# Threshold attention and SwiGLU on one core: the first batch's planned order, its spread, and the opening scores

## The chip, the cores and the metric

The kernel runs on one core of a Trainium2 chip. The metric is the device time of one execution in microseconds (us). The kernel before took 1339.34 us (median of 3 runs, 1338.71 to 1340.52). The core's engines each work through an instruction queue of their own: TensorE (PE in the profile, its weight loads PEld), VectorE (DVE), ScalarE (ACT) and GpSimd (POOL); SyncE (SP) issues most of the DMAs. They meet only at semaphores.

## What is computed

Eight batches of eight heads, 576 tokens, head dimension 64. Per head, scores below the row's maximum less tau are masked out; then softmax and the product with v. The 4608 x 512 result goes through a SwiGLU block with d_ff = 1536. Cut from the reference:

```python
scores = scale * np.matmul(q, k.transpose(0, 1, 3, 2))
thresh = np.max(scores, axis=-1, keepdims=True) - tau
scores = np.where(scores >= thresh, scores, -1000000000.0)
scores = scores - np.max(scores, axis=-1, keepdims=True)
attn = np.exp(scores)
attn = attn / (np.sum(attn, axis=-1, keepdims=True) + 1e-09)
x = np.matmul(attn, v)          # then heads side by side: (4608, 512)
g = x @ w_gate
out = (g * (1.0 / (1.0 + np.exp(-g))) * (x @ w_val)) @ w_out
```

All of it is float32.

## The kernel before, in words

The work has three stages.

**The first batch, order written out by hand (0 to about 130 us).** Heads go in four pairs. For each pair the queries are cut in tiles of 128 rows: first two early tiles of each pair, then the rest (two of 128 rows and a last one of 64). The loop at L801 runs over pairs and tiles. `scores` (L489) is a generator: it issues the score products of both heads of a tile (`sc`, L498; keys of all 576 tokens, two PSUM banks for a head), takes each row's maximum on VectorE (L515, `nm`), yields, has ScalarE form threshold and exponential (L518, L519), yields, has VectorE mask and sum (L522), add up (L524) and invert (L525, `ri`), and scales. `flip_steps` (L549) then turns the tile on TensorE (`tp`, `end`, L568 and L572), ScalarE copies it out (L575, L582), and `attend_tile` (L586) multiplies by v (`xa`). The pool `ps_s` has room for the scores of one tile (two buffers of two banks); the other four banks are the pool `ps_f`, handed out in turn by `bank` (L292). `run_idle` (L301) issues products whose result nobody reads, before the first scores and again while the first tile is on the other engines.

Ahead of that loop, L749 to L754 set up the inputs: tau's DMA is issued on ScalarE's queue, then `fetch_qk(0)` issues four loads of k and four of q, five on SP and three on ScalarE's queue; a load takes one of eight semaphores in turn, and one whose semaphore is in use waits for the load that holds it. `prepare` (L717) transposes k, scales the first queries by a factor formed from tau, and transposes them.

Between the tiles, pieces of the weights are loaded and turned into a two-part form (`split_weights`, `shift_weights`, `join_weights`; L361, L362 on ScalarE; L381, L388 on VectorE; L398 on GpSimd).

**Batches two to eight, order set by a planner (from about 127 us).** `Plan` (L28) keeps an assumed time for TensorE (`plan.t`) and for every other engine (`plan.free`). Each piece of work on VectorE, ScalarE, GpSimd or SP is a job with an engine, an assumed duration, jobs that it waits for, a rank, and possibly a lag (time after its end until others can go on). The planner issues jobs in the order in which they could start by these times; so the assumed times set only the order of the instructions in each queue. TensorE's own order is written out. `take` (L919) picks the bank that comes free first by the plan. `shares` (set at L2423, for the tail alone) makes the planner stretch jobs of VectorE and GpSimd that run side by side, by the factors `SLOWED` (L34).

Attention here goes in slots: each pair has three, so a batch has 12 (slots s = 0 to 11 are batch two, 12 to 23 batch three). `slot_scores` issues 64 small products in one block (L2088; about 1.65 us, both buffers of `ps_s`), and `slot_rest` makes the jobs behind them: maxima (L2109, L2111), exchange between row groups on ScalarE (L2123) or on VectorE (L2117) by a table, threshold (L2130), exponentials (L2134), masks (L2136), sums (L2145, L2151), inverse (L2152), scaling on ScalarE (L2164) or GpSimd (L2161), transposes (L2166). The next block of scores needs the banks that the last masks release. After three slots `attend` (L2188) multiplies by v. Between the blocks of scores TensorE works on the SwiGLU block of the batch before; for the first batch that is `plain_group` (L1400: `pg`, `pv`), which goes in steps of four 128x128x256 products. Tables say how many steps go into which slot and who does what: `PLAIN` and `CH0` for batch two, `GV_FIRST` for batch three, `FIRST_POOLED` (how many of a slot's scalings go to GpSimd) and `FIRST_MAX_BY_ACT` (whose exchange is done by ScalarE) for both. `rest_of_weights` (L960) makes jobs of the weight pieces that are not done by then (L982, L985 on ScalarE; L992, L994 on VectorE; L996 on GpSimd), with an assumed landing time `landed` for loads that are already on their way.

The hand-over is in the loop at L2369: at s = 0 the last tile of the first stage is finished by hand, and then the plan's clocks are set:

```python
plan.t += 2.4
plan.free.update(DVE=2.0, ACT=2.5)
```

**The tail (from about 1130 us).** The last gate and value products come from `Whole` (L2574: `pa`, `pb`, `pe`, `sc` by bank), in twelve groups, then the output products from `Deep` (L1797, L1806). A gate's seven partial products are copied by ScalarE or added by VectorE (`Seven.fill`, L1300 and L1302; L2646, L2656) and folded by four additions on GpSimd or VectorE (`Seven.fold`, L1304); then come Tanh on ScalarE (L2624), a multiply on VectorE (L2626), and the gate's multiply.

Of the kernel before, what the change touches and what calls it, by code (L numbers as in the profile page):

```python
# [10 lines left out]
F32 = mybir.dt.float32  # L11
# [3 lines left out]
ALU = mybir.AluOpType  # L15
# [12 lines left out]
class Plan:  # L28
# [2 lines left out]

    HOP, PIPE = 0.08, 0.22
    PATIENCE = 0.2
    SLOWED = {"DVE": 0.45, "POOL": 0.2}  # L34
    AGE = 12.0

    def __init__(self):
# [120 lines left out]
def kernel(  # L158
# [40 lines left out]
    qkp = ctx.enter_context(tc.tile_pool(name="qkp", bufs=2))  # L199
    stp = ctx.enter_context(tc.tile_pool(name="stp", bufs=4))  # L200
    ps_s = ctx.enter_context(tc.tile_pool(name="ps_s", bufs=2, space=bass.MemoryType.PSUM))
    ps_f = ctx.enter_context(tc.tile_pool(name="ps_f", bufs=1, space=bass.MemoryType.PSUM))
    hbm = ctx.enter_context(tc.tile_pool(name="hbm", bufs=1, space=bass.MemoryType.DRAM))
    ctx.enter_context(tc.manual_schedule())

# [92 lines left out]
    def give_back(ps):  # L298
        turns.append(taken.pop(id(ps))[0])

    def run_idle(n):  # L301
        ps = bank("idle")
        for _ in range(n):
            nc.tensor.matmul(ps[:, 0:TC], ones[:, 0:P], ones, start=True, stop=True)
        give_back(ps)

    FW = 384
    TW = 2 * FW
# [177 lines left out]
    def statistics(*names):  # L486
        return [stp.tile([P, 2 * NU3, 2] if x == "mx" else [P, 2 * NU3], F32, name=x) for x in names]

    def scores(seg, t):  # L489
        qT, kT = seg["qT"], seg["kT"]  # L490
        q0 = t * P - seg["q0"]
        if t < NT:
            pss = [ps_s.tile([P, 2, 512], F32, name="sc") for _ in range(2)]
            for h, hs in enumerate(heads):
                cut_ = D if turned(t) and h == 1 else 0
                for n, lo, to in [(0, 0, D), (0, D, SH), (1, 0, SH)] if cut_ else [(0, 0, SH), (1, 0, SH)]:
                    at_ = (n * SH + lo - cut_) % S
                    nc.tensor.matmul(pss[h][:, n, lo:to], qT[hs, q0:q0 + P], kT[hs, at_:at_ + to - lo],  # L498
                                     start=True, stop=True)
        else:  # L500
            pss = [ps_s.tile([P, 2, 512], F32, name="sc")]
            for n, h in ((0, 0), (1, 1), (1, 0), (0, 1)):
                hs = heads[h]
                nc.tensor.matmul(pss[0][hs, n, 0:SH], qT[hs, q0:q0 + D], kT[hs, n * SH:(n + 1) * SH],
                                 start=True, stop=True)
        nm, th, ri, tot = statistics("nm", "th", "ri", "tot")
        sm = sums[0]
        sums.rotate(1)
        m = len(pss)
        scs = [ps[:, :, 0:SH] for ps in pss]  # L510
        both = pbufs[0].rearrange("p h s -> p (h s)")[:, KM:KM + P]
        ps = [pbufs[0][:, x, :].rearrange("p (n s) -> p n s", n=2) for x in range(m)]
        pbufs.rotate(1)
        for x in range(m):
            nc.vector.tensor_reduce(out=nm[:, x:x + 1], in_=scs[x], axis=AX.XY, op=ALU.max, negate=True)  # L515
        yield
        for x in range(m):
            nc.scalar.activation(th[:, x:x + 1], nm[:, x:x + 1], AF.Identity, bias=cut, scale=-1.0)  # L518
            nc.scalar.activation(ps[x], scs[x], AF.Exp, bias=nm[:, x:x + 1])  # L519
        yield  # L520
        for x in range(m):
            nc.vector.scalar_tensor_tensor(out=ps[x], in0=scs[x], scalar=th[:, x:x + 1], in1=ps[x],  # L522
                                           op0=ALU.is_ge, op1=ALU.mult, accum_out=sm[:, x, 0:1])
        nc.vector.tensor_reduce(out=tot[:, 0:m], in_=sm[:, 0:m, 0:3:2], axis=AX.X, op=ALU.add)  # L524
        nc.vector.reciprocal(out=ri[:, 0:m], in_=tot[:, 0:m])  # L525
# [220 lines left out]
        ready.append(unit)  # L746
        left[0] += cost(unit)

    run_idle(6)  # L749
    nc.scalar.dma_start(out=tau_s, in_=tau.partition_broadcast(P))  # L750
    fetch_qk(0)
    prepare(segs[0])
    fetch_qk(1)
    nc.scalar.activation(junk, minus2, AF.Exp)  # L754
# [31 lines left out]
    def steps(n, x, point):  # L786
        for what in STEPS.get((n, x, point), ()):
# [9 lines left out]
            else:  # L797
                {"scale": scale_next, "turn": turn, "split": split_weights, "shift": shift_weights,
                 "join": join_weights}[what]()

    for n, seg in enumerate(segs[:2 * NP]):  # L801
        early_slots[0] = n < NP
        if n >= NP:
            seg["v"] = segs[seg["i"]]["v"]
        for x, t in enumerate(seg["tiles"]):
            assert n < NP or seg["i"] in turned_rests
            go = scores(seg, t)
            next(go)
            steps(n, x, "maxima")
            if n >= NP:  # L810
                join_weights(1)
            if not n and not x:
                run_idle(6)
            next(last, None)
            box = []
            if n < NP:
# [45 lines left out]
            gates()  # L862
            last = go
            steps(n, x, "end")
            if n >= NP and x == len(seg["tiles"]) - 2 and n + 1 < len(segs):
                prepare(segs[n + 1])

# [92 lines left out]
    def rest_of_weights():  # L960

        todo = [(dst, None, place, lo) for dst, place, lo in split] + [(dst, None, place, None) for dst, place in fetched]
        landed = 6.3
        todo += [(dst, srcs, place, None) for dst, srcs, place in wpieces]
        done, joins = {}, []
        for n, (dst, srcs, place, lo) in enumerate(todo):
# [323 lines left out]
    class Seven(Buf):  # L1290
# [13 lines left out]
        def fold(self, eng, rank, *deps):  # L1304

            y = self.place.rearrange("p (x q) -> p x q", q=P)
            tt, took, less = (dve_tt, 0.36, 0.23) if eng == "DVE" else (pool_tt, 0.73, 0.46) if tail[0] else (pool_tt, 0.75, 0.44)
            twice = lambda x: y[:, x:x + 1].broadcast_to((P, 2, P))
            j = job(eng, took, tt(y[:, 1:3], twice(0), y[:, 1:3], ALU.add), *deps, rank=rank)
            j = job(eng, took, tt(y[:, 0:7:6], twice(2), y[:, 5:7], ALU.add), j, rank=rank)  # L1310
            j = job(eng, less, tt(y[:, 2], y[:, 0], y[:, 3], ALU.add), j, rank=rank)
            return job(eng, took, tt(y[:, 4:6], twice(6), y[:, 4:6], ALU.add), j, rank=rank, lag=0.3 if tail[0] else 0.0)

    class Flat:

# [988 lines left out]
    LAST_GV, LAST_PLAIN, LATE_V = 9, 8, 10  # L2304
    HELD = 4
    GV = {1: 3, 2: 6, 3: 4, 4: 6, 5: 7, 6: 3, 7: 5, 8: 7, 9: 0}
    GV_FIRST = {1: 5, 2: 8, 3: 2, 4: 5, 5: 7, 6: 2, 7: 5, 8: 7, 9: 0}
    CH = {0: 2, 1: 3, 10: 4, 11: 4}
    POOLED = {NS: 2, 0: 3, 1: 1, 2: 1, 3: 3, 4: 3, 5: 2, 6: 1, 7: 2, 8: 1}
    MAX_BY_ACT = (0, 1, 3, 4, 5, 6, 8, 9)  # L2310
    FIRST_POOLED = {0: 2, 4: 1, 5: 1, 8: 1, 9: 1, 11: 2, 12: 2, 13: 3, 15: 3, 16: 3, 17: 2, 19: 2, 20: 2, 22: 3, 23: 3}
    FIRST_MAX_BY_ACT = (1, 3, 6, 9, 10, 11, 12, 13, 14, 18, 20, 21)
    CD = {0: 1, 1: 1, 9: 2, 10: 2, 11: 2}
    PLAIN = {0: 3, 1: 5, 2: 6, 3: 2, 4: 5, 5: 5, 6: 3, 7: 3}
    CH0 = {7: 1, 8: 3, 9: 2, 10: 3, 11: 3, 12: 2}

    def begin_outputs(c):
# [51 lines left out]
    for s, (n, x) in enumerate((n, x) for n in range(len(halved)) for x in range(NU3)):  # L2369
# [6 lines left out]
        if s == 0:  # L2376
# [1 line left out]
            attend_tile()  # L2378
            next(last, None)
            flip()  # L2380
            plan.t += 2.4
            plan.free.update(DVE=2.0, ACT=2.5)
        elif s == 1:
            box = []
            m = pe(1.0, lambda: attend_tile(lambda *y: box.extend(y)))
# [358 lines left out]
```

## Time and profile before

| what | us |
|---|---|
| runs of the kernel before (3) | 1338.71, 1339.34, 1340.52 |
| the profiled execution's own time | 1340.89 |
| its span, first to last instruction | 1338.8 |
| TensorE with a running matmul | 1324.7 (99%) |
| VectorE, GpSimd, ScalarE busy | 1095.3, 940.2, 900.5 |
| from the first instruction to the first score products | 7.88 |
| first score products to the first block of slot scores | 7.88 to 126.77 |
| granted TensorE clock, mean | 0.999 |

The profile shows one execution. A row of the timeline tells when a group of equal instructions began (us from the span's start), how long it took in all, its engine, its line, what it writes and reads, how many they were, and in brackets how long the engine had been idle before and what ended that. A matmul of 128x256 in float32 runs as two passes, and each pass is a row of the trace: at full clock a pass of 256 columns starts every 0.216 us, and one of 128 columns every 0.112 us. The end of a matmul is modelled, so for a pause I look at the distance between starts. The view of stretches gives, for each stretch of time, what every engine was busy and the granted clock.

### The profile page before, as it was taken

How to read it: one execution, taken by the hardware profiler on the slowest of the kernel's cores; microseconds unless marked ns; L12 is line 12 of the kernel's file. 1: busy time of each engine (PE TensorE's matmuls, PEld its weight loads, DVE VectorE, ACT ScalarE, POOL GpSimd, SP SyncE). 2: the span in 40 equal slices, each digit the busy share in tenths (PEclk: the TensorE clock that was granted, in tenths of full speed). 3: DMA queues.
4: the chain of work that ended last, by engine and by line, in shares of the span. 5: the costliest groups of instructions: out<-in, count | busy, mean ns of one | idle time of the engine just before them, and what ended most of it. 6: DMA issues, size and time to landing. Idle time of an engine off the chain costs nothing. (4 is left out here: it accounts for less than half of the span.)

```text
span 1338.8 us, 41744 instructions
## 1 busy us (share of the span) xinstructions
PE 1324.7 (99%) x16298; PEld 1122.5 (84%) x16298; DVE 1095.3 (82%) x2904; ACT 900.5 (67%) x2345; POOL 940.2 (70%) x1124
## 2 busy tenths in 40 slices
PE   8999999999999999999999999999999999999998
PEld 6777777787887888888888888888888888999998
DVE  6889898888887788888888887888788888767886
ACT  6898776767755777787677777777777774444300
POOL 2588497565685969857895779677975798866720
PEclk9999999999999999999999999999999999999999
DMA  8753424356557653656365736655475627565341
GB/s 183 198 193 96 81 60 133 123 150 178 154 167 217 174 172 94 198 170 220 76 201 170 233 103 188 186 164 154 110 218 142 217 69 226 160 199 185 96 170 40
DMA packets 230884, 209.81 MB, mean 157 GB/s; under 512 B 167968, under 2 KB 185376, under 8 KB 223008
## 3 DMA queue, kind: packets, MB, share of 16 engines
q1 hardware_dynamic: 226768, 206.22, 52.2%
q8 instruction: 129, 2.11, 0.6%
q10 hardware_dynamic: 3920, 0.92, 0.3%
q14 instruction: 67, 0.55, 0.1%
HBM read 169.08 MB, written 38.01 MB: 155 GB/s over the span
## 5 line engine op out<-in xcount | busy, mean ns | idle before, releaser
L2136 DVE SCALAR_TENSOR_TENSOR pall<-sc,th,pall 128x288 f32<-128x288 f32 x504 | 244.1, 514 | 39.9 <-ACT pall L2134 20.8
L2134 ACT ACTIVATE pall<-sc,nm 128x288 f32<-128x288 f32 x504 | 232.6, 497 | 35.0 <-DVE pall L2136 34.8
L1167 PE MATMUL pb<-xall,big 128*128 128x256 f32 x864 | 205.9, 381 | 0.0
L2166 DVE STREAM_TRANSPOSE pall<-pall 128x576 f32<-128x576 f32 x252 | 188.0, 763 | 19.8 <-ACT pall L2164 9.8
L948 POOL TENSOR_TENSOR big<-big 128x128 f32<-128x128 f32 (+3 forms) x226 | 168.0, 752 | 50.9 <-ACT big L1302 22.1
L2164 ACT ACTIVATE pall<-pall,ri 128x288 f32<-128x288 f32 x386 | 178.3, 527 | 26.0 <-DVE ri L2152 25.0
L1167 PEld LDWEIGHTS pb<-xall,big 128*128 128x128 f32 x864 | 161.4, 190 | 23.6 <-issue 2.2
L948 POOL TENSOR_TENSOR hall<-hall,tmp 128x512 f32<-128x512 f32 x80 | 102.2, 1279 | 86.7 <-DVE hall L1226 66.9
L2109 DVE TENSOR_REDUCE mx<-sc 128x2 f32<-128x576 f32 x168 | 125.7, 748 | 41.9 <-PE sc L2088 41.6
L2088 PE MATMUL sc<-kT,qT 64*32 64x288 f32 (+1 forms) x5376 | 145.3, 345 | 1.1 <-DVE pall L2136 1.1
L1167 PE MATMUL pa<-xall,big 128*128 128x256 f32 x576 | 137.8, 382 | 0.0
L2088 PEld LDWEIGHTS sc<-kT,qT 64*32 64x32 f32 x5376 | 96.0, 106 | 49.4 <-issue 8.6
L2188 PE MATMUL xa<-pall,vall 64*32 64x288 f32 x4032 | 128.7, 404 | 0.0
L1167 PEld LDWEIGHTS pa<-xall,big 128*128 128x128 f32 x576 | 108.0, 190 | 17.2 <-issue 2.5
L2188 PEld LDWEIGHTS xa<-pall,vall 64*32 64x32 f32 x4032 | 74.0, 107 | 46.9 <-issue 4.3
L2161 POOL TENSOR_SCALAR pall<-pall,ri 128x288 f32<-128x288 f32 x118 | 59.4, 514 | 51.9 <-DVE ri L2152 51.6
L2145 ACT COPY sums<-sums 32x6 f32<-32x6 f32 x336 | 66.6, 198 | 29.2 <-DVE pall L2136 24.0
L1167 PE MATMUL pe<-xall,big 128*128 128x256 f32 x352 | 83.9, 381 | 0.0
L2111 DVE TENSOR_REDUCE mx<-sc 128x1 f32<-128x288 f32 x168 | 75.0, 447 | 0.0
L1167 PEld LDWEIGHTS pe<-xall,big 128*128 128x128 f32 x352 | 66.4, 190 | 10.2 <-ACT xlast L2200 0.7
L948 POOL TENSOR_TENSOR hall<-hall 128x384 f32<-128x384 f32 (+2 forms) x69 | 70.3, 1035 | 0.8
L948 POOL TENSOR_TENSOR big<-hall 128x384 f32<-128x384 f32 (+2 forms) x69 | 65.6, 974 | 4.3 <-PE pa L1167 4.2
(401 smaller groups left out, 3062.1 us busy)
## 6 DMA issues: line engine op xcount, KB each, us to landing
big<-sums_hbm SPq DMA_DIRECT2D x30, 1280.0 KB, 7.5
big<-sums_hbm SPq DMA_DIRECT2D x30, 1024.0 KB, 7.3
vall<-in_v_dram SPq DMA_DIRECT2D x112, 144.0 KB, 4.0
big<-sums_hbm SPq DMA_DIRECT2D x54, 256.0 KB, 3.4
sums_hbm<-big SPq DMA_DIRECT2D x36, 256.0 KB, 3.6
out_dram<-big SPq DMA_DIRECT2D x32, 256.0 KB, 3.0
qT<-in_q_dram SPq DMA_DIRECT2D x112, 72.0 KB, 4.2
kT<-in_k_dram SPq DMA_DIRECT2D x112, 72.0 KB, 3.0
```

The costliest lines, as they stand in the source:

```text
L948: nc.gpsimd.tensor_tensor(out=out, in0=a, in1=b, op=op)
L1167: nc.tensor.matmul(ps[:, i], w[:, k_, i * P:(i + 1) * P], x[:, k_, :], start=first and i == k_ == 0, stop=True, skip_group_check=True)
L2088: nc.tensor.matmul(pss[h][(slice(g * G, (g + 1) * G), *part)], qT[hs, col:col + G], kT[hs, c * SH + keys[0]:c * SH + keys[1]], start=True, ...
L2109: rs.append(job("DVE", 0.72, lambda n=n, tile_=tile_: nc.vector.tensor_reduce(out=mx[:, n:n + 2, 0], in_=tile_[:, :, 0:SH], axis=AX.X, op= ...
L2111: rs.append(job("DVE", 0.42, lambda n=n, tile_=tile_: nc.vector.tensor_reduce(out=mx[:, n + 2:n + 3, 0], in_=tile_[:, :, SH:SH + SQ], axis ...
L2134: ej = job("ACT", 0.42, lambda x=x, n=n: nc.scalar.activation(ps[x], scs[x], AF.Exp, bias=nm[:, n:n + 1]), ej, masks.get((h, u - 1)), rank=0)
L2136: masks[x] = job("DVE", 0.45, lambda x=x, n=n: nc.vector.scalar_tensor_tensor(out=ps[x], in0=scs[x], scalar=th[:, n:n + 1], in1=ps[x], op0 ...
L2145: nc.scalar.copy(sm[g * G:(g + 1) * G, 0:m, 1], sm[o * G:(o + 1) * G, 0:m, 0])
L2161: scaled.append(job("POOL", 0.48 if seg["i"] >= 3 * NP else 0.4, lambda x=x, n=n: nc.gpsimd.tensor_scalar(out=x, in0=x, scalar1=ri[:, n:n ...
L2164: scaled.append(job("ACT", 0.46, lambda x=x, n=n: nc.scalar.activation(x, x, AF.Copy, scale=ri[:, n:n + 1]), rj, rank=rank))
L2166: seg["turned"].append(job("DVE", 0.72, lambda both=both: nc.vector.transpose(out=both, in_=both), *scaled, rank=rank))
L2188: nc.tensor.matmul(holds[a].ap()[x * G:(x + 1) * G, 0:SH].rearrange("d (i q) -> d i q", q=G), vr[rs, h, j, ds], p[rs, h, :, j, :], start=( ...
```

## The change

Six edits.

1. **Opening.** The pool `ps_f` is opened only after the first tile. Until then its four banks hold the scores of the first tile (`first_pool`), so that the first two tiles have banks of their own. The scores of the second tile are issued right behind those of the first; its maxima are taken when its turn comes (`later`). The idle products write to a part of the first tile's bank that the scores leave free: 224 columns wide instead of 256, six and then four instead of six and six.
2. **Maxima.** In `scores`, a maximum is issued right behind its head's products instead of behind both heads'.
3. **Loads.** `fetch_qk(0)` comes ahead of tau's DMA.
4. **Hand-over.** The plan's clocks are set to other values, GpSimd's too, and the two banks that were given back last are marked as busy until ScalarE's assumed time. The loads on their way are assumed to land at 8.0 instead of 6.3.
5. **Spread.** The tables `PLAIN`, `GV_FIRST`, `FIRST_POOLED` and `FIRST_MAX_BY_ACT` get other entries.
6. **Tail.** The lag of a fold is 0.6 instead of 0.3, and the factor of GpSimd beside VectorE 0.3 instead of 0.2.

The diff, cut to its core:

```diff
-    SLOWED = {"DVE": 0.45, "POOL": 0.2}
+    SLOWED = {"DVE": 0.45, "POOL": 0.3}
...
-    ps_f = ctx.enter_context(tc.tile_pool(name="ps_f", bufs=1, space=bass.MemoryType.PSUM))
...
-    def run_idle(n):
-        ps = bank("idle")
+    def run_idle(n, ps):
         for _ in range(n):
-            nc.tensor.matmul(ps[:, 0:TC], ones[:, 0:P], ones, start=True, stop=True)
-        give_back(ps)
+            nc.tensor.matmul(ps[:, 1, SH:512], ones[:, 0:P], ones[:, 0:512 - SH], start=True, stop=True)
...
-    def scores(seg, t):
+    def scores(seg, t, pss=None, later=False):
...
+        def maximum(x):
+            nc.vector.tensor_reduce(out=nm[:, x:x + 1], in_=pss[x][:, :, 0:SH], axis=AX.XY, op=ALU.max, negate=True)
...
+                if not later:
+                    maximum(h)
...
+        yield
...
-        for x in range(m):
-            nc.vector.tensor_reduce(out=nm[:, x:x + 1], in_=scs[x], axis=AX.XY, op=ALU.max, negate=True)
+        if later or t >= NT:
+            for x in range(m):
+                maximum(x)
         yield
...
-    run_idle(6)
+    first_pool = tc.tile_pool(name="first", bufs=1, space=bass.MemoryType.PSUM)
+    in_first = first_pool.__enter__()
+    first_pss = [in_first.tile([P, 2, 512], F32, name=f"first{h}") for h in range(2)]
+    run_idle(6, first_pss[0])
+    fetch_qk(0)
     nc.scalar.dma_start(out=tau_s, in_=tau.partition_broadcast(P))
-    fetch_qk(0)
...
+    begun = deque([scores(segs[0], 0, first_pss)])
...
-            go = scores(seg, t)
+            go = begun.popleft() if begun else scores(seg, t)
+            if (n, x) != (0, 1):
+                next(go)
+            if (n, x) == (0, 0):
+                begun.append(scores(seg, seg["tiles"][1], later=True))
+                next(begun[0])
             next(go)
...
-                run_idle(6)
+                run_idle(4, first_pss[0])
...
+            if not n and not x:
+                first_pool.__exit__(None, None, None)
+                ps_f = ctx.enter_context(tc.tile_pool(name="ps_f", bufs=1, space=bass.MemoryType.PSUM))
...
-        landed = 6.3
+        landed = 8.0
...
-            return job(eng, took, tt(y[:, 4:6], twice(6), y[:, 4:6], ALU.add), j, rank=rank, lag=0.3 if tail[0] else 0.0)
+            return job(eng, took, tt(y[:, 4:6], twice(6), y[:, 4:6], ALU.add), j, rank=rank, lag=0.6 if tail[0] else 0.0)
...
-    GV_FIRST = {1: 5, 2: 8, 3: 2, 4: 5, 5: 7, 6: 2, 7: 5, 8: 7, 9: 0}
+    GV_FIRST = {1: 5, 2: 8, 3: 2, 4: 5, 5: 7, 6: 2, 7: 6, 8: 6, 9: 0}
...
-    FIRST_POOLED = {0: 2, 4: 1, 5: 1, 8: 1, 9: 1, 11: 2, 12: 2, 13: 3, 15: 3, 16: 3, 17: 2, 19: 2, 20: 2, 22: 3, 23: 3}
-    FIRST_MAX_BY_ACT = (1, 3, 6, 9, 10, 11, 12, 13, 14, 18, 20, 21)
+    FIRST_POOLED = {0: 2, 1: 2, 4: 1, 5: 1, 6: 2, 8: 1, 9: 2, 11: 3, 12: 3, 13: 3, 15: 3, 16: 3, 17: 2, 19: 2, 20: 2, 22: 3, 23: 2}
+    FIRST_MAX_BY_ACT = (1, 2, 3, 6, 9, 10, 11, 12, 14, 15, 17, 20, 21)
...
-    PLAIN = {0: 3, 1: 5, 2: 6, 3: 2, 4: 5, 5: 5, 6: 3, 7: 3}
+    PLAIN = {0: 4, 1: 4, 2: 6, 3: 3, 4: 4, 5: 5, 6: 3, 7: 3}
...
-            plan.t += 2.4
-            plan.free.update(DVE=2.0, ACT=2.5)
+            plan.t += 1.8
+            plan.free.update(DVE=2.7, ACT=4.4, POOL=5.7)
+            for n_ in list(turns)[-2:]:
+                j = Job("ACT", 0.0, None, 0, 0.0, 0.0)
+                j.end = plan.free["ACT"]
+                banks[n_].jobs.append(j)
```

More of the change, by code (lines that the diff above doesn't have):

```diff
@@ L487, in statistics @@
         return [stp.tile([P, 2 * NU3, 2] if x == "mx" else [P, 2 * NU3], F32, name=x) for x in names]
-    def scores(seg, t):
+    def scores(seg, t, pss=None, later=False):
         qT, kT = seg["qT"], seg["kT"]
         q0 = t * P - seg["q0"]
+        nm, th, ri, tot = statistics("nm", "th", "ri", "tot")
+        def maximum(x):
+            nc.vector.tensor_reduce(out=nm[:, x:x + 1], in_=pss[x][:, :, 0:SH], axis=AX.XY, op=ALU.max, negate=True)
         if t < NT:
-            pss = [ps_s.tile([P, 2, 512], F32, name="sc") for _ in range(2)]
+            pss = pss or [ps_s.tile([P, 2, 512], F32, name="sc") for _ in range(2)]
             for h, hs in enumerate(heads):
@@ L505, in scores @@
                                  start=True, stop=True)
-        nm, th, ri, tot = statistics("nm", "th", "ri", "tot")
+        yield
         sm = sums[0]
```

## The prediction

> **What bounds the kernel now.** I read the page first: is one engine full all the way, or does each stretch have its own limit?
>
> ```profile
> PE 1324.7 (99%) x16298; PEld 1122.5 (84%) x16298; DVE 1095.3 (82%) x2904; ACT 900.5 (67%) x2345; POOL 940.2 (70%) x1124
> ```
>
> TensorE is the bound: 14.1 us of the 1338.8 are without a running matmul. So a change is worth only the TensorE pauses that it closes (and the slow matmuls before the clock rises). Next I read TensorE's rows of the timeline for pauses of over 0.3 us, and the rows of the other engines around each. Three places are touched by the diff.
>
> *The start* (timeline, 0 to 40 us; columns: start, time, engine, line):
>
> ```profile
> 7.88 2.13 PE L498 MATMUL sc<-pall,qT 64*128 64x288 f32 x8 [2.05 <-DVE cap L734]
> ...
> 9.94 3.62 PE L304 MATMUL idle<-pall 128*128 128x256 f32 x12
> 10.02 1.42 DVE L515 TENSOR_REDUCE nm<-sc 128x1 f32<-128x576 f32 x2 [1.77 <-PE sc L498]
> ...
> 13.49 1.27 PE L498 MATMUL sc<-pall,qT 64*128 64x288 f32 x8
> 13.63 0.17 DVE L525 RECIPROCAL ri<-tot 128x2 f32<-128x2 f32 x1
> ...
> 14.76 1.42 DVE L515 TENSOR_REDUCE nm<-sc 128x1 f32<-128x576 f32 x2 [0.96 <-PE sc L498]
> ...
> 18.05 1.94 PE L498 MATMUL sc<-pall,qT 64*128 64x288 f32 x8 [0.94 <-DVE pall L522]
> ```
>
> TensorE fills 9.94 to 13.56 with idle products, because the second tile's scores need banks that the first tile's masks release only at 13.4. So VectorE, done with tile one at 13.80, waits 0.96 us for tile two, and the scores of tile three (18.05) wait on that chain.
>
> *The hand-over to the planner* (timeline, 123 to 144 us):
>
> ```profile
> 130.93 0.22 ACT L582 COPY big<-end 128x64 f32<-128x64 f32 x1
> ...
> 131.21 3.72 PE L1400 MATMUL pg<-xall,big 128*128 128x256 f32 x16 [0.58 <-ACT big L582]
> ...
> 134.73 0.93 ACT L982 ACTIVATE wo<-xall 128x768 f32<-128x768 f32 x1 [1.14 <-DMA xall<-in_moe_w_out_dram]
> ...
> 137.61 0.52 DVE L2136 SCALAR_TENSOR_TENSOR pall<-sc,th,pall 128x288 f32<-128x288 f32 x1
> 137.75 2.14 PE L2088 MATMUL sc<-kT,qT 64*32 64x288 f32 x64 [1.10 <-DVE pall L2136]
> ```
>
> The planner's first bank is the one that ScalarE is still emptying, and slot two's scores wait for slot one's last masks, late since a weight step (L982) sat in ScalarE's queue for a load that landed at 134.71.
>
> *The tail* (timeline, 1245 to 1257 us):
>
> ```profile
> 1251.61 0.63 ACT L2624 ACTIVATE kT<-xall 128x512 f32<-128x512 f32 x1 [1.96 <-POOL xall L948]
> 1252.15 0.47 ACT L1300 ACTIVATE tmp<-sc 128x384 f32<-128x384 f32 x1
> 1252.52 0.59 ACT L1302 ACTIVATE tmp<-sc 128x512 f32<-128x512 f32 x1
> ...
> 1253.16 0.71 PE L2574 MATMUL sc<-xall,big 128*128 128x128 f32 x4 [0.68 <-ACT tmp L1302]
> ```
>
> A Tanh waits 1.96 us for GpSimd's fold, and the two copies that TensorE needs stand behind it.
>
> **Part by part.**
>
> *Second tile's scores at once.* Built order: TensorE now issues both tiles' scores, then 4 idle products; tile two's maxima have no wait left. They start at 13.80 instead of 14.76: −0.96. All that follows keeps that distance: from 18 to 57 us ScalarE is 96% busy and TensorE 99%, so no pause is there to swallow it, and the first 20 weight pieces have landed 2.8 us or more before their use, the later ones are issued by events that move along. The two heads' scores run side by side (their rows start 13 ns apart), so taking each maximum straight after its head gains nothing. Idle products: 8 passes instead of 12, hidden under VectorE's 10.02 to 13.80.
>
> *q sooner, tau later.* ScalarE's queue issues k, k, q, tau instead of tau, k, k, q: each 0.45 us earlier, tau some 1.6 us later. But what started the first scaling of q (6.99) was the fourth q piece on SP, landed 6.91, and in the built order it still waits for the first k to land (4.02). The nine landings are 0.3 to 0.65 us apart whatever the queue, so it keeps its place, or gains the 0.33 of one place (the other pair's k, asked for later now). The other end: tau lands 0.2 us after q and the scaling waits for it. I take −0.1 (range −0.4 to +0.3). Behind that wait stand VectorE's scaling and transpose, and for them the first scores.
>
> *Hand-over.* The two banks just given back are now marked busy, and the first product takes the bank that the value step (VectorE, done 128.64) left: −0.80 (131.21 against 130.41, when the transposes' end is issued). Slot one gets 4 steps instead of 3 (a step is 8 passes of 0.216 = 1.73 us), and the weight step moves behind the last exponentials. TensorE reaches slot two's scores at 130.41 + 2 × 3.46 = 137.33; without L982 ahead of them the masks end at about 137.2 (exponentials 0.45, masks 0.45 each from 133.86 on, one Tanh of 0.59 between). So the 1.26 (1.10 idle and a last product drawn out) goes, and the 0.43 by which that block of scores was longer than the usual 1.64: −1.69. Together −2.49.
>
> *What is late next.* The products only move, so some slots get thin: slot two 1.65 + 0.89 + 4 steps = 9.5 us, slot five 8.7 (4 steps instead of 5). A slot's masks end 8.7 to 10.0 us after its scores start (8.72 in the slot from 213.53, 10.02 in that from 137.75). In slot two VectorE's order now has a transpose of k ahead of the totals and the next maxima; its load lands at 139.02, and all of them queue behind. I take +0.5 there, +0.3 in slot five, −0.1 for slot four, which becomes fat: +0.7 (range 0 to +2.0). More scaling by GpSimd (6 more of 0.5 us in 24 slots) hides: it is 62 to 76% busy there.
>
> *Tail.* A longer lag for folds and a dearer GpSimd put the copies ahead of that Tanh, and likewise in the place with the second pause (1164.67, 0.37). Both pauses, 0.84 + 0.37 = 1.21, could go; the Tanh, its multiply and the gate come up to 1.1 us later, and banks are handed out anew. Otherwise TensorE has no pause from 1134 on. I take −0.8 (range −1.2 to +1.5). A pause of 1.2 us at 1130.81 that no semaphore explains stays.
>
> **Sum:** −0.96 − 0.1 − 2.49 + 0.7 − 0.8 = −3.65 us. The profiled execution took 1340.89 us (span 1338.8 and 2.1 around it), 1.55 above the median of the runs, 1339.34; from the median: **1335.7 us**.
>
> **The clock, row and rule.** Stretches cut at the clock's steps (columns: stretch, length, busy of PE, PEld, DVE, ACT, POOL, granted clock, DMA):
>
> ```profile
> 4.69:8.11 3.42, 1.37 (x7) 0.89 (x8) 1.83 (x7) 1.48 (x2) 0.00 (x0) 1.00 0.90 136
> 8.11:11.52 3.41, 3.41 (x12) 2.15 (x11) 1.56 (x3) 0.71 (x3) 0.48 (x1) 0.50 0.95 283
> ...
> 14.93:18.35 3.42, 2.48 (x21) 2.11 (x21) 3.42 (x7) 2.80 (x8) 0.00 (x0) 1.00 0.85 114
> ```
>
> A stretch with TensorE 40% busy (1.37 of 3.42) is followed by half clock, one with 73% by full clock. After the change TensorE is done with the idle products at about 13.3 and pauses to 14.69: its stretch 11.52 to 14.93 is about 60% busy, between the two rows. The Trainium skill, "TensorE: Matmul & The Clock Gate", Part 1, has the clock fall after an idle window of about 3.4 us, so by it this pause costs nothing. The trace has the clock fall after a pause of 2.05 us, so here the row decides.
>
> **Rivals.**
> - *The clock falls back* at 14.93. For: 60% is nearer to 73 than to 40, but not above it. The flip's 20 passes then take 0.213 instead of 0.112: tile three's scores start at about 18.3 instead of 17.1. Cost 1.25: −2.4, 1336.9 us. Chance 0.14.
> - *Thin slots eat the gain.* For: slot two's and five's budgets above are below the chains of most neighbours. Against: slots of 9.60 ran without a pause. At +2.0, and with a tail that gains nothing: −0.96 − 0.1 − 2.49 + 2.0 = −1.55, 1337.8 us. Chance 0.22.
> - *The tail's order turns against it* (slower). The copies now go first and the Tanhs are late; if the late gates hold the banks' next products as the fold did (0.84 each), seven of the tail's twelve groups cost +5.9: −2.85 + 5.9 = +3.05, 1342.4 us; it decides from four waits on. Against: each group repeats, and ten of twelve had no such wait. Chance 0.07.
> - *q isn't sooner*: as worked out, that is nearly my own case; it costs 0.1.
>
> **How the numbers follow.** My forecast has 0.57. Measurement tells 0.2%, 2.7 us, from no change: below 1336.7 is faster. Faster 0.57; the clock and the thin slots fall within it: 0.36; slower 0.07. Extremes of the terms: −1.4 − 2.5 + 0 − 1.2 = −5.1 on one side, on the other the thin-slot case with another 1.0 for tail or clock: −0.5. Range 1334.2 to 1338.8.
>
> **What would show it.** Right: tile two's maxima directly behind the reciprocal and tile three's scores about 1.0 us earlier; granted clock 1.00 from 11.5 on; no pause at the planner's first product; slot two's scores at about 136.3 instead of 137.75, with one step more behind them; no pause of over 0.3 us from 1134 on. Wrong: a half-clock stretch after 14.9, pauses of over 0.5 us ahead of slot three's or six's scores, or new ones in the tail.

## The result, and the profile after

The changed kernel took **1335.42 us** (median of 8 runs, 1333.69 to 1336.99) beside 1339.49 for the kernel before (8 runs, 1338.71 to 1340.67): ratio 0.997, 95% interval 0.9961 to 0.9979. The forecast was 1335.7 and "faster", with a range of 1334.2 to 1338.8. A second set of 9 runs, made with the last experiments, gave 1336.33 beside 1339.47: 0.9973 (0.9963 to 0.9982). So the time was foreseen; of the terms it was made of, only some were.

The profiled execution of the changed kernel is one of its fastest: 1334.49 us, span 1332.7, which is 6.1 less than the profiled span of before. That pair of traces puts the 6.1 here (how much sooner TensorE reaches the same product than before; the starts in the views are rounded):

| up to | sooner, us | of this, gained here |
|---|---|---|
| first block of slot scores (125.78, before 126.77) | 0.98 | 0.98 |
| the block that stood at 149.49 | 3.23 | 2.25 |
| the block that stood at 301.2 | 3.59 | 0.36 |
| the block that stood at 421.3 | 4.01 | 0.42 |
| the end of attention (1124) | 4.00 | 0 |
| the last output products | 6.06 | 2.06 |

(The block at 149.49 is the first after the hand-over ahead of which both kernels have done the same steps.) The 0.42 before 421 is a pause of that one execution: the kernels with the opening alone, the tail alone and the lag alone, told below, keep everything between 140 and 1130 us as it was and lack it too.

The page of the changed kernel, engines:

```profile
PE 1320.4 (99%) x16294; PEld 1119.3 (84%) x16294; DVE 1092.1 (82%) x2900; ACT 898.7 (67%) x2343; POOL 945.1 (71%) x1130
```

TensorE has 12.3 us without a running matmul, 1.8 fewer than before. Its matmuls also run 4.3 us less in all, and 2.5 of these lie ahead of tile three's scores (11.26 us busy up to 16.86, before 13.73 up to 18.05): there are 20 idle passes of 224 columns instead of 24 of 256, and the first scores and idle products of before ran in part at half clock.

*The start.* Timeline of the changed kernel, 0 to 20 us (L500, L302, L492, L524, L530, L573 are L498, L304, L515, L519, L525, L568 of before):

```profile
6.90 1.25 PE L500 MATMUL first<-pall,qT 64*128 64x288 f32 x8 [0.75 <-DVE cap L739]
...
8.17 1.42 DVE L492 TENSOR_REDUCE nm<-first 128x1 f32<-128x576 f32 x2 [0.91 <-PE first L500]
...
9.14 1.78 PE L302 MATMUL first<-pall 128*128 128x224 f32 x8
...
10.96 0.74 ACT L524 ACTIVATE pall<-first,nm 128x576 f32<-128x576 f32 x1 [1.70 <-PE first L302]
...
13.60 0.17 DVE L530 RECIPROCAL ri<-tot 128x2 f32<-128x2 f32 x1
...
13.69 1.40 DVE L492 TENSOR_REDUCE nm<-sc 128x1 f32<-128x576 f32 x2
...
14.32 2.05 PE L573 MATMUL tp<-pall 128*128 128x128 f32 x16 [3.40 <-ACT pall L543]
...
16.86 1.97 PE L500 MATMUL sc<-pall,qT 64*128 64x288 f32 x8
```

Tile two's maxima do follow the reciprocal directly (13.60, 13.69). But the first scores start 0.98 sooner than before and take 1.25 instead of 2.13, and still the reciprocal is where it was (13.63). What ate 1.85 us is in the fourth row: the first exponential waits 1.70 us for the idle products, which now write to the tile that it reads. And TensorE stands still for 3.40 us ahead of 14.32.

*The hand-over.* Timeline of the changed kernel, 122 to 147 us (L1417, L587 and L2105 are L1400, L582 and L2088 of before):

```profile
129.57 3.72 PE L1417 MATMUL pg<-xall,big 128*128 128x256 f32 x16
129.95 0.22 ACT L587 COPY big<-end 128x64 f32<-128x64 f32 x1
...
136.67 1.72 PE L2105 MATMUL sc<-kT,qT 64*32 64x288 f32 x64
```

The first product no longer waits for ScalarE's copy; it starts ahead of it. The block of scores that stood at 137.75 with a pause of 1.10 has none, with one step more ahead of it. In slots two to five no pause of 0.3 us or more is left.

*The tail.* TensorE's rows with an idle time, 1120 us to the end, are three before:

```profile
1130.81 0.60 PE L1797 MATMUL px<-wo,hall 128*128 128x128 f32 x3 [1.03 <-issue]
1164.67 0.71 PE L2574 MATMUL pb<-xall,big 128*128 128x128 f32 x4 [0.21 <-ACT tmp L1302]
1253.16 0.71 PE L2574 MATMUL sc<-xall,big 128*128 128x128 f32 x4 [0.68 <-ACT tmp L1302]
```

In the changed kernel they are one (L1814 is L1797 of before):

```profile
1127.05 0.38 PE L1814 MATMUL px<-vends,hall 128*128 128x128 f32 x2 [0.49 <-issue]
```

The pauses that are 0.37 and 0.84 by the distance of starts are gone; the one that no semaphore explains is half as long.

### The profile page after: what moved, and what is told of

Read it like the earlier page. It is cut to its first block, busy times and chain, and to the rows that moved or that the text cites. A ratio compares the mean times of both kernels' runs of the same rounds, so it can differ in the third digit from the quotient of the medians.

```text
span 1332.7 us, 41737 instructions
## 1 busy us (share of the span) xinstructions
PE 1320.4 (99%) x16294; PEld 1119.3 (84%) x16294; DVE 1092.1 (82%) x2900; ACT 898.7 (67%) x2343; POOL 945.1 (71%) x1130
## 4 chain that ended last, share of the span: by engine, by line
PE 94%; ACT 3%; POOL 1%; DMA 1%; DVE 1%; issue 0%; SPq 0%; ACTq 0%; DVEq 0%
PE pb L1184 14%; PE px L1814 12%; PE sc L2105 10%; PE pa L1184 10%; PE xa L2205 10%; PE pe L1184 6%; PE po L1492 6%; PE sc L2595 5%; PE py L1814 4%; PE pe L1379 3%; PE pb L2595 2%; PE pg L1417 2%; PE pa L2595 2%; PE pv L1417 2%; PE py L1823 2%; PE sc L500 1%
## 5 line engine op out<-in xcount | busy, mean ns | idle before, releaser
L2105 PE MATMUL sc<-kT,qT 64*32 64x288 f32 (+1 forms) x5376 | 144.1, 345 | 0.0
L2105 PEld LDWEIGHTS sc<-kT,qT 64*32 64x32 f32 x5376 | 95.0, 106 | 48.1 <-issue 8.3
L2178 POOL TENSOR_SCALAR pall<-pall,ri 128x288 f32<-128x288 f32 x124 | 63.9, 528 | 48.4 <-DVE ri L2169 48.1
```

What stands on the lines that cost most here:

```text
L2105: nc.tensor.matmul(pss[h][(slice(g * G, (g + 1) * G), *part)], qT[hs, col:col + G], kT[hs, c * SH + keys[0]:c * SH + keys[1]], start=True, ...
```

## Experiments

Two theories of the opening stand against each other. *The prediction's*: edit 1 is worth −0.96 and edit 3 next to nothing. *From the trace after*: edit 3 brings about 1 us, and edit 1 loses it again by the exponential's wait, and perhaps by the clock over its pause. For the rest the question is which part of edits 4 to 6 gains what.

**Each group of edits alone.**

Opening alone (edits 1 to 3 on the kernel before):

> The kernel before with the opening alone (edits 1 to 3). By the prediction: tile two's maxima directly behind tile one's reciprocal, -0.96, and q -0.1, so the first block of slot scores at 125.7 instead of 126.77 and the run about 1.06 us shorter than before. Rival, from the trace of the changed kernel: there the first scores already began 0.98 us sooner (6.90 instead of 7.88), and the first exponential then waited 1.70 us for the idle products; if it is the loads that bring the sooner start, this kernel shows it too, tile one's reciprocal stands at about 13.6 all the same, and the whole gain is again about 1.0. If the sooner start was chance, the first scores stand at about 7.9, the idle products end at about 12, and tile one ends 0.9 later: no gain.

Measured: 1339.44 us (11 runs) beside 1339.58: ratio 1.0003 (0.9994 to 1.0012), no gain. Its profiled execution is as the rival says: first scores at 6.99, reciprocal at 13.69, first block of slot scores at 125.84. But the whole gain of about 1.0 that the rival took from it is missing in the median as well. Of its 11 runs 8 have a mean clock below 1.00; the second run of the changed kernel, further down, shows what that costs.

Hand-over and spread alone (edits 4 and 5 on the kernel before):

> The kernel before with the hand-over and the spread alone (edits 4 and 5). By the prediction: -2.49 at the hand-over, +0.7 in thin slots: 1.8 us shorter. By the trace of the changed kernel, if these edits alone do it: the block of slot scores at 149.5 comes 2.25 us sooner, no pause in thin slots, another 0.25 gained between 250 and 300 us and 0.42 at about 421 us: 3.0 us shorter up to 1108 us, and the tail as before. If the 0.25 and the 0.42 came from the earlier opening, this kernel stays at 2.3.

Measured: 1336.42 us (11 runs), ratio 0.9978 (0.9969 to 0.9987): −3.2. In its trace 2.25 us are gained between the first block and that at 149.5, and 0.25 by 301 us, as in the changed kernel; of the 0.42 before 421 only 0.19. So neither the gain at the hand-over nor the 0.25 hangs on the opening.

Tail alone (edit 6 on the kernel before):

> The kernel before with the tail's two numbers alone (edit 6). By the prediction: both pauses of 0.37 (1164.67) and 0.84 (1253.16) can go, -0.8 taken, the pause of 1.2 at 1130.81 stays. By the trace of the changed kernel: both pauses go entirely, -1.21, and the pause at 1130.81 is a matter of chance or of what runs beside it: between 0 and -0.65 more. Rival: the tail's order needs the rest of the change; then a pause of over 0.3 remains.

Measured: 1337.37 us (11 runs), ratio 0.9985 (0.9976 to 0.9994): −2.2. In its trace both pauses are gone, and the unexplained one stands at 0.58 (starts: 0.75 over the usual distance, before 1.20). From the end of attention to the last output products 1.87 us are gained.

These two kernels keep the opening of before, and in their profiled executions it ran at full clock from the first scores on. Timeline of the kernel with the tail alone, 4 to 20 us:

```profile
7.83 1.25 PE L498 MATMUL sc<-pall,qT 64*128 64x288 f32 x8 [1.49 <-DVE cap L734]
...
9.10 1.42 DVE L515 TENSOR_REDUCE nm<-sc 128x1 f32<-128x576 f32 x2 [0.91 <-PE sc L498]
...
12.71 0.17 DVE L525 RECIPROCAL ri<-tot 128x2 f32<-128x2 f32 x1
...
13.06 1.57 DVE L515 TENSOR_REDUCE nm<-sc 128x1 f32<-128x576 f32 x2 [0.19 <-PE sc L498]
13.76 2.05 PE L568 MATMUL tp<-pall 128*128 128x128 f32 x16
```

This is the row that decides the prediction's first step. At full clock tile two's maxima wait 0.19 us, not the 0.96 of the profiled execution of before, whose scores and idle products ran at half clock from 8.11 to 11.52. All eight profiles without edits 1 and 2 agree, with the loads in either order: 0.64 to 1.00 in the four with such a stretch, 0.18 or 0.19 in the four without. The old opening reaches the first block of slot scores at 125.40 then, 0.4 *ahead* of the new one.

**The opening, taken apart.**

The order of loads alone (edit 3 on the kernel before):

```diff
-    nc.scalar.dma_start(out=tau_s, in_=tau.partition_broadcast(P))
     fetch_qk(0)
+    nc.scalar.dma_start(out=tau_s, in_=tau.partition_broadcast(P))
```

> The kernel before with the order of the loads alone (edit 3: q's and k's loads ahead of tau's). By the prediction it gains 0.1, since the fourth q piece on SP keeps its place. By the traces so far (first scores at 6.84 to 6.99 with the new order, 7.83 to 7.88 with the old one, the rest of the opening unchanged here) all of the opening comes 0.95 us sooner: first scores at 6.9, tile one's reciprocal at 11.8, the first block of slot scores at 124.4 and the run 0.95 shorter than before. Then the other parts of the opening (edit 1) would be worth +1.4 us by themselves, since with them that block starts at 125.8.

Measured: 1338.38 us (11 runs) beside 1339.40: ratio 0.9991 (0.9982 to 1.0). In its profiled execution the scaling of q waited for q until 6.68, and a stretch of half clock followed, so that the first block stood at 126.5 there; the next kernel shows the places expected.

The changed kernel with edits 1 and 2 undone:

> The changed kernel with edits 1 and 2 undone: the old pool, second tile's scores behind the idle products, both maxima behind both heads; the new order of loads, the hand-over, the spread and the tail stay. Theory: edit 1 loses more by its new wait and its pause than it gains: here tile one's reciprocal stands at about 11.8 instead of 13.60, the first block of slot scores at 124.4 instead of 125.8 at full clock, the pause of 2 us ahead of the first scores halves the clock in a quarter to 40% of the runs only; the median is 1.2 to 2 us below the changed kernel's, 1333.5 to 1334.2. Rival, the prediction's: edit 1 is worth -0.96; the median is about 1 us above the changed kernel's.

Measured: 1333.63 us (5 runs, 1333.28 to 1334.39), ratio 0.9954 (0.9941 to 0.9968); the changed kernel beside it took 1336.33 (9 runs, none under 1334.86). Reciprocal at 11.73, first block of slot scores at 124.27. The prediction's −0.96 for edit 1 falls: it costs 1.5 us by the traces (124.27 against 125.78) and 2.7 by these medians.

The changed kernel with its idle products in another bank:

```diff
-                run_idle(4, first_pss[0])
+                run_idle(4, second[0])
```

(`second[0]` is the other bank pair of the second tile's scores, whose readers come later.)

> The changed kernel, with the four idle products behind the scores written into the bank of the second tile instead of the first's. Theory: in the changed kernel the first exponential waits 1.70 us for the idle products only because they write to the tile that it reads; here it starts at about 9.3 instead of 10.96, and everything behind it up to the first slot comes 1.7 us sooner; the first block of slot scores at 124.1 instead of 125.79, the run 1.7 us shorter than the changed kernel. Rival one: the second pair's keys (turned at 15.00 in the changed kernel) and the values are then not there; the gain is cut to 0.5 or less by waits on loads. Rival two: TensorE now pauses from about 10.7 to 12.6 with no work and the granted clock drops to 0.5 for a stretch of 3.4 us, which costs 1.2 of the 1.7.

Measured: 1333.04 us (5 runs, 1332.21 to 1333.90), ratio 0.9951 (0.9939 to 0.9964), the shortest of all kernels tried. Timeline, 4 to 20 us (line numbers up to 4 higher than in the changed kernel):

```profile
9.09 1.78 PE L302 MATMUL sc<-pall 128*128 128x224 f32 x8
9.11 0.72 ACT L528 ACTIVATE pall<-first,nm 128x576 f32<-128x576 f32 x1
...
11.73 0.17 DVE L534 RECIPROCAL ri<-tot 128x2 f32<-128x2 f32 x1
...
12.45 2.05 PE L577 MATMUL tp<-pall 128*128 128x128 f32 x16 [1.58 <-ACT pall L547]
```

The exponential starts with the idle products instead of behind them, 1.85 sooner; the first block of slot scores stands at 124.02, 1.76 sooner; TensorE's pause has shrunk from 3.40 to 1.58. A load takes part of it back at one place. Timeline, 133 to 160 us (PEld: the weight loads of the block of slot scores):

```profile
136.36 0.78 DVE L2259 STREAM_TRANSPOSE kT<-kT 128x576 f32<-128x576 f32 x1 [0.66 <-DMA kT<-in_k_dram]
...
144.49 0.14 PEld L2109 LDWEIGHTS sc<-kT,qT 64*32 64x32 f32 x2 [0.33 <-issue]
144.91 1.42 PEld L2109 LDWEIGHTS sc<-kT,qT 64*32 64x32 f32 x62 [0.28 <-PE pv L1421]
```

VectorE waits 0.66 for the load of k with slot two's maxima queued behind, and the next block stands 0.42 after its first two products. That is the prediction's thin slot; in the changed kernel, 1.8 us later, the load is there in time. Of the 1.76, 1.35 are left one block further on.

The changed kernel without those idle products:

```diff
-                run_idle(4, first_pss[0])
+                pass
```

> The changed kernel without the four idle products behind the scores (nothing that is computed is left out). Both theories of the exponential's wait: it starts at about 9.2 and tile one's reciprocal is at 11.7, as with the idle products in the other bank. They differ in the clock. Theory: a pause of TensorE of over 3 us (here 9.2 to 12.4) makes the granted clock fall in most runs, as the pause from 10.92 to 14.32 did in six of eight runs of the changed kernel (mean clocks 0.997 to 0.999): most runs have a mean clock under 1.00, the median stands 1 to 2 us above that of the kernel with the idle products in the other bank, 1334 to 1335. Rival: those clocks came from elsewhere in the run, and the idle products are not needed: clock 1.00 in all runs, the same 1333.

Measured: 1333.19 us (5 runs, 1333.10 to 1336.02), ratio 0.9959 (0.9946 to 0.9971). Four of five runs have a mean clock of 0.998 or 0.999, as the first theory has it, but the median is not 1 to 2 us above that of the kernel just told; the one run at 1.00 is the longest (no profile shows why; a slow start, told with the last kernel, would not show in its mean). Only the profiled pair shows a price (first block at 125.02 against 124.02). With five runs each, the price in the median stays open.

The changed kernel once more:

> The changed kernel once more, unchanged, beside the next three. Theory of the clock: its pause of 3.40 us (10.92 to 14.32) lies across the clock's stretches of 3.41 us as chance has it, and a stretch in which TensorE is busy for 41% or less is followed by half clock (40, 41, 40 and 11% were; 44, 45, 55 and 57% were not). Then about four runs in five have a mean clock of 0.999 or less, and these are about 1 us longer than those at 1.00. Rival: the clocks below 1.00 of the first eight runs were chance; then at least half of the runs stand at 1.00, as most runs of the kernel before do.

Measured: 1336.33 us; 8 of 9 runs below a clock of 1.00, and the one at 1.00 is the shortest, 1334.86. Over both sets 14 of its 17 runs are below 1.00 (median 1336.22) and three at it (1334.49); of the 73 runs of the kernel before that the experiments brought, 50 are at 1.00 (median 1339.27) and 23 below (1340.50). So runs with a stretch at half clock are 1.2 us longer in the kernel before and 1.7 in the changed one, and the changed kernel meets it in four runs of five, the kernel before in one of three. In this profiled execution the trace shows it. Stretches at the clock's steps (stretch, length, busy of PE, PEld, DVE, ACT, POOL, granted clock, DMA):

```profile
13.84:17.25 3.41, 1.28 (x11) 1.28 (x12) 3.34 (x9) 2.06 (x7) 0.00 (x0) 1.00 0.87 147
17.25:20.67 3.42, 3.42 (x17) 2.73 (x18) 2.27 (x8) 3.04 (x6) 0.24 (x1) 0.50 0.84 255
```

The same view of the first profiled execution of the changed kernel, where no fall came:

```profile
9.40:12.80 3.40, 1.52 (x8) 1.17 (x7) 1.26 (x4) 1.56 (x3) 0.00 (x0) 1.00 1.03 278
12.80:16.20 3.40, 1.88 (x16) 1.86 (x16) 3.33 (x9) 2.33 (x7) 0.00 (x0) 1.00 0.99 236
```

And of the kernel without idle products:

```profile
9.36:12.78 3.42, 0.38 (x3) 0.38 (x4) 3.02 (x9) 2.07 (x7) 0.00 (x0) 1.00 1.06 287
12.78:16.19 3.41, 3.41 (x20) 3.10 (x18) 3.17 (x9) 2.34 (x6) 0.00 (x0) 0.50 1.13 262
```

The clock of a stretch follows TensorE's busy share of the one before: 38% (1.28 of 3.41) and 11% are followed by half clock, 45% and 55% are not. In the first 25 us of all 14 profiles, from the first stretch at full clock on, none of 41% or less kept the clock and none of 44% or more lost it. The pause of 3.40 is as long as a stretch, and where the stretches begin differs from run to run: the first profiled execution happened to have the pause cut nearly in half (1.88 idle in one, 1.52 in the next).

**The hand-over, taken apart.**

Without the marks on the two banks (on the kernel with edits 4 and 5 alone):

```diff
-            for n_ in list(turns)[-2:]:
-                j = Job("ACT", 0.0, None, 0, 0.0, 0.0)
-                j.end = plan.free["ACT"]
-                banks[n_].jobs.append(j)
```

> The kernel before with the hand-over and the spread (edits 4 and 5), but without marking the two banks given back last as busy. By the prediction the marks are worth 0.80: the planner's first product waits again for ScalarE's copy of the end and starts 0.8 later than with them (129.9 instead of 129.13 in the trace with them), and so does the next block of slot scores: the run is 0.8 longer. Rival: that block is held by the masks of the slot before anyway (they ended at 135.97, it started at 136.23), so that only about 0.3 to 0.5 is lost; or the other plan clocks already choose another bank, and nothing is lost.

Measured: 1337.10 us (10 runs), ratio 0.9984 (0.9975 to 0.9993), 0.7 above the kernel with the marks, which is within the noise of the medians. In the trace the stretch from the first block of slot scores to the next takes 0.66 longer. From that block to the one after it takes 2.15 less than before, as with the marks; 1.73 of these are the step that now stands in the slot ahead.

Without the tables (edit 4 alone on the kernel before):

> The kernel before with the hand-over's clocks, marks and landing alone (edit 4), the four tables as before. With the tables this came to -3.16 in the medians, and in the trace -2.25 up to the block at 149.5 and another -0.25 between 250 and 300 us. Theory: the pauses at the hand-over go by the clocks and marks, but with three steps in slot one the next scores, due by TensorE at about 134.5, wait for masks that end at about 136: some 1.5 us of pause come back there, the run is 1.0 to 1.5 shorter than before instead of 3.2. Rival: the masks follow closer, and the tables gain nothing: 2.5 to 3 shorter.

Measured: 1340.63 us (11 runs), ratio 1.001 (1.0001 to 1.0018): longer than before, and 4.2 above the kernel with the tables. Timeline, 122 to 170 us:

```profile
134.18 1.89 PE L1400 MATMUL pv<-xall,big 128*128 128x256 f32 x8
137.08 2.14 PE L2088 MATMUL sc<-kT,qT 64*32 64x288 f32 x64 [1.01 <-DVE pall L2136]
...
149.22 2.14 PE L2088 MATMUL sc<-kT,qT 64*32 64x288 f32 x64 [0.34 <-DVE pall L2136]
```

The first product starts in time (130.62), but with three steps in slot one TensorE is through them 0.6 us sooner than before and waits for the masks all the same (1.17 by the starts); another 0.50 is lost at 149.22 and 0.90 at 167.96. Both theories of this run were too kind to it: without the tables, the clocks and marks are worth nothing. The tables without the clocks, and the four tables apart, weren't tried.

**The tail, taken apart.** The fold's lag alone (0.6, GpSimd's factor as before):

> The kernel before with the fold's lag of 0.6 alone (half of edit 6). Theory: the lag moves the copies ahead of the Tanh, and both pauses of the tail go: 1.2 to 1.9 us sooner at the end of the tail, as with both numbers. Rival: the order of GpSimd beside VectorE does it (0.3 instead of 0.2); then a pause of over 0.3 us remains here.

Measured: 1339.07 us (10 runs), ratio 0.9997 (0.9988 to 1.0006). TensorE's rows with an idle time, 1120 us to the end:

```profile
1129.11 0.60 PE L1797 MATMUL px<-wo,hall 128*128 128x128 f32 x3 [0.84 <-issue]
1163.15 0.71 PE L2574 MATMUL pb<-xall,big 128*128 128x128 f32 x4 [0.39 <-ACT tmp L1302]
1269.96 1.60 PE L1797 MATMUL sc<-wo,hall 128*128 128x128 f32 x12 [0.24 <-ACT pall L1820]
```

The lag removes the 0.84 at 1253. The pause at 1163 stays (0.56 by the starts), and one of 0.40 comes at 1269.96. Only with the factor too are all three gone; the factor alone wasn't tried.

**A further version.** On the kernel with the idle products in the other bank, one step moved from slot three to slot two:

```diff
-    PLAIN = {0: 4, 1: 4, 2: 6, 3: 3, 4: 4, 5: 5, 6: 3, 7: 3}
+    PLAIN = {0: 4, 1: 5, 2: 5, 3: 3, 4: 4, 5: 5, 6: 3, 7: 3}
```

> The changed kernel with the idle products in the second tile's bank, and one step moved from slot three to slot two (5 and 5 instead of 4 and 6), since with the earlier opening the block of slot scores at 144.50 stood 0.42 us for masks that were late through a wait of 0.66 for the load of k ahead of the maxima. Theory: those 0.42 go, nothing else moves: 0.4 less than the kernel with the idle products in the other bank, about 1332.6, clock 1.00 in all runs. Rival: slot three gets thin in its place, and its next scores wait; the same 1333.0.

Measured: 1333.65 us (5 runs), ratio 0.9955 (0.9943 to 0.9968): not shorter. Timeline of its profiled execution (1335.27 us, the longest of the five), 4 to 14 us:

```profile
6.89 2.30 PE L504 MATMUL first<-pall,qT 64*128 64x288 f32 x8 [0.72 <-DVE cap L743]
8.97 1.99 PE L504 MATMUL sc<-pall,qT 64*128 64x288 f32 x8
```

The first scores take 2.30 instead of 1.25, the pace of half clock, and so everything behind them is 1.05 us later (first block at 125.07). The granted clock of the views is 1.00 in these rows and in the mean of this run: it doesn't show the slow pace with which all 14 profiles begin (the first seven idle passes of 224 columns take 2.98 us; eight take 1.78 at full clock), and which lasted until about 10.5 here and in the second profile of the changed kernel (first scores 2.30 there too). So the mean clock misses one kind of loss. With the later start k's load is in time anyway, so that the place was not tested; pauses of 0.76 and 0.38 came ahead of 165.68 and 179.29, in later slots. The best version found is the one with the idle products in the second tile's bank, 6.5 us under the kernel before in the medians; the one with edits 1 and 2 undone (1333.63), the one without idle products (1333.19) and this one can't be told from it.

## Why the prediction was right in its time and wrong in its terms

| term | predicted | measured |
|---|---|---|
| second tile's scores at once (edits 1, 2) | −0.96 | +1.5 (traces, full clock from the first scores on), +2.7 with the clock (medians) |
| q sooner (edit 3) | −0.1 | −1.0 (medians), −1.1 (traces, 124.27 against 125.34) |
| hand-over, and thin slots | −2.49 + 0.7 | −2.25 up to 149.5, −0.25 behind; −3.2 in the median |
| tail | −0.8 | −1.4 in the stretch with the two pauses (1.2 of pause), −0.45 to −0.65 at the unexplained one; −2.2 in the median |
| sum | −3.65 | −4.07 (first set), −3.14 (second) |

*Second tile's scores: wrong.* The step that failed is "They start at 13.80 instead of 14.76: −0.96". The wait was real in the profiled execution, but most of it was the half-clock stretch's work; at full clock it is 0.19, and two of three runs of the kernel before run at full clock. The step also left out that the idle products' new place is a place that another engine reads; the row to ask for was "who waits for this line" at the new idle products. That the straight maximum gains nothing was right (first scores to maxima: 1.27 in both). The sign that was set for this step came true all the same, with tile three's scores at 16.86 instead of 18.05. But without edit 1 they stand at 16.50 at full clock with the old loads, and at 15.52 with the new, so the sign could not tell the step from these.

*The clock: the rival that came true, in four runs of five.* I gave it 0.14, and put the place at 60% of a stretch. The row used (40% falls, 73% holds) was sound, and in these 14 profiles the bound lies between 41 and 44%. What was wrong is that the stretches' places in the profile of before were taken as fixed, where each run has others, and that the pause came out at 3.40 instead of some 1.4. The Trainium skill, "TensorE: Matmul & The Clock Gate", Part 1, says of the window that it has 3413 ns and runs freely, so that the same kernel differs from run to run: the stretches of 3.41 to 3.42 us and their changing places agree. By its other rule, that the clock falls after an idle window of about 3.4 us, a pause of 2.05 would be harmless; the trace of before differs, and the measurement decides.

*q sooner: the step was mis-sized.* "Nine landings 0.3 to 0.65 us apart whatever the queue" took tau's load for one more of nine. But with it in front the loads behind are slower. The DMA view, 0 to 8 us in slices of 0.2 (mean busy share of the 16 DMA engines in tenths, and what they moved), kernel before:

```profile
DMA  0000000005256799999987769984389998869997
GB/s 0 0 0 0 0 0 0 0 3 96 43 73 95 112 142 178 210 215 212 189 131 105 88 104 164 176 106 58 52 141 191 212 177 125 131 103 164 152 158 107
```

and the changed kernel:

```profile
DMA  0000000007899999999723367899999999969389
GB/s 0 0 0 0 0 0 0 0 6 125 140 164 211 207 205 209 209 195 170 76 29 55 43 95 113 126 150 153 172 183 205 207 177 149 176 95 142 40 146 125
```

From 1.8 to 3.0 us the loads run at 43 to 142 GB/s with tau ahead and at 125 to 211 without it; the first keys are turned at 4.79 instead of 5.74 (4.79 to 4.97 in the eight profiles with the new order, 5.72 to 5.76 in the six with the old). Part of it is that ScalarE issues its first load of k at 0.74 instead of 1.20; but SP's queue, which tau's load isn't in, has moved less by 3.0 us too (0.09 MB instead of 0.12, ScalarE's queue 0.02 instead of 0.09). What 0.5 KB does beyond the later issue wasn't tried apart.

*Hand-over: right in kind.* The bank's pause is worth 0.66 where 0.80 was taken, and the first of the blocks starts at 136.67 (136.23 with the old opening at full clock) where 136.3 was foreseen, though edit 4 alone has no gain: the pause at the scores goes only when the tables add a step ahead of it. *Thin slots* cost nothing here (+0.7 was taken); the mechanism shows only with an opening that is earlier still (VectorE waits for k's load 0.66 with the idle products in the other bank, 0.51 with edits 1 and 2 undone and 0.97 without the idle products, and 0.42, 0.27 and 0.73 of the lead over the changed kernel is lost within two blocks).

*Tail: right in kind.* Both pauses went, so that the caution of 0.4 was not needed, and the unexplained pause, said to stay, differs from run to run: 0.49 idle in one profile of the changed kernel and under 0.25 in the other, 0.42 to 1.24 in ten of the 14 profiles and under 0.25 in four. Its cause stays open. The slower rival did not come.

So the time was met by luck: an opening that gained nothing, where 1.06 was taken, stood against 1.8 (traces) to 2.8 (medians) more than was taken from the other two. The parts alone add up to −0.1 − 3.2 − 2.2 = −5.5, the whole is −4.07 and −3.14; each of these medians has an interval of over 1 us to either side, so that an interaction is neither shown nor excluded.

## What to carry to other kernels

Before you price a wait of a profiled execution, ask what the clock was in it, and whether other executions had the same: a wait that hangs on half clock is no property of the kernel. When work moves to another buffer, list who reads that buffer: filler that nobody reads still makes a reader wait. And try a plan's clocks and its tables as one edit: of the 3.2 us at the hand-over, the clocks alone gave none.

## What the runs showed of the hardware

The granted clock changes at the ends of stretches of 3.41 us, and in 14 profiles it fell after stretches with TensorE busy for 41% or less and held after those of 44% or more; where the stretches lie differs from profile to profile. A kernel with one pause of 3.40 us had a mean clock below 1.00 in 14 of 17 runs, the three kernels with no such pause (1.58 us the longest behind the first scores in their profiles) in none of 15; a slow start, as in one of those 15, isn't in that mean. All of this was seen in the first 25 us only. With one small load (0.5 KB to 128 rows) issued ahead of ScalarE's share of the first eight, the first keys were ready 0.95 us later.
